# A cross-attention and MoE kernel on one core: first loads in four parts, states in two, and a new order of steps

## The chip, the cores and the metric

The kernel runs on one core of a Trainium2 chip. The metric is the device time of one execution in microseconds; several runs are made, and their median is compared.

## What is computed

Eight batches of x (8 heads, 512 tokens, 64 wide) and of a state (8 heads, 32 rows, 64 wide) attend to each other in both directions, and the two reads, laid one after the other, go through a two-layer network with a leaky activation:

```python
# x: (8, 8, 512, 64), state: (8, 8, 32, 64)
scores  = x @ state.T / 8;    xread = softmax(scores) @ state     # tokens read the states
scores2 = state @ x.T / 8;    sread = softmax(scores2) @ x        # states read the tokens
rows = concat([xread, sread], tokens)                             # (8 * 544, 512)
h = rows @ w_in                                                   # 512 -> 2048
g = max(h, 0) + alpha * min(h, 0)
out = g @ w_out                                                   # 2048 -> 512
```

## The kernel before

TensorE (PE) is given every matmul, VectorE (DVE), ScalarE (ACT) and GpSimd (POOL) share the rest, and SyncE (SP) issues most DMAs. Each engine works through its own list in order. These lists are written out in full: the text `ORDER` (lines 18 to 99) holds some 1,100 steps, a name and its numbers with points between, and the loop at lines 767 to 769 calls the function of each step in turn. A step's letters name its engine (`a`, `v`, `p`), and a last digit from 0 to 5 names the PSUM bank (one of six) that its result takes.

**The weights of the first product are folded into the states.** Since xread = a @ state, rows @ w_in = a @ (state @ w_in). A step `m.b.f` (line 517) multiplies batch b's states by the f-th quarter of w_in, and `mo` copies it out as f16. A step `F.b.jc` (line 550) is then one of 16 groups of 128 columns of h for the 512 tokens of batch b: two matmuls of 128 x 512. `N.b.jc` (line 606, ScalarE) takes relu(-h), `G.b.jc` (line 611, VectorE) adds (1 - alpha) times that to h, which gives g. Batch 8 in these names is the states' own rows.

**The second product.** For batch 0 it is plain: `S.0.q.j` (line 619) is two matmuls of 128 x 512 of output rows q, and `O` stores them. For batches 1 to 8 it is one level of a Strassen-like scheme with seven products: `P.b.p.i.c` (line 707) is four matmuls of 128 x 256 of product p, `U.b.i.c` (line 683, GpSimd) makes the sums of g that products 3, 5, 6 and 7 need, `W` the sums of the weights, `K` keeps a partial result, `Q.b.th.dh` (line 741) adds and stores a quarter; its output tiles `osb` have four buffers.

**Attention.** `sc` computes the scores of a batch with the states on the rows, `tm` the maximum over tokens, `te` the exponential, `tn` the norm, `tt` the transposition by DMA on SP, `rd` and `rdo` the states' reads. `sb` (line 346) transposes the scores in blocks of 32, `smax`, `ssh`, `sexp`, `ssum`, `snorm` and `wb` make the tokens' softmax, which `F` multiplies. For batches 2 to 7 `lx` loads x through GpSimd's queue with a cast to f16 and `xd` transposes it by DMA; for batches 0 and 1 TensorE transposes it (`xt`, copied out by `xo`).

**The opening.** Batch 0 goes in two halves of tokens, j = 0 and 1. `load_x0` loads each half as f32 on SP's queue, two DMAs of 512 KB; four steps `cx.j.g` cast a half's four heads to f16. `tsc` computes token scores of batch 0 directly, from the block-diagonal `st_pairs` that `sbd` fills; `at` and `ao` transpose the finished weights. `stc`, `stt`, `sto` cast, transpose and copy out batch 0's states; `lst` loads the states of batches 1 to 7 with one DMA, `str.i` transposes half i of them (0: batches 1 to 4's front part, 1: the rest), `sro.i` copies it out. `oma` transposes alpha and takes 1 - alpha. The first four column groups of batch 0 are computed by half: `f.0.pair.j`, four matmuls of 256, `n`, and `g` twice. `Z.k.n` (line 232) is a fill: n matmuls on a constant pattern into bank k whose result nothing reads. `wi` and `wo` load quarters of w_in and w_out through GpSimd's queue.

Of the kernel before, what the change touches and what calls it, by code (L numbers as in the profile page):

```python
# [29 lines left out]
S.0.3.3 F.0.9.4 m.1.2 F.0.12.1 ssh.p.1 sexp.1 G.0.10 S.0.2.5 S.0.1.5 ssum.1.s N.0.9 G.0.9 F.0.13.3 S.0.3.5 mo.1.2.a  # L30
m.1.3 N.0.12 G.0.12 S.0.3.4 F.0.15.4 tn.1.1.a N.0.13 G.0.13 F.0.14.1 S.0.1.4 S.0.3.6 S.0.1.6 W.2.0.p S.0.2.4 N.0.15
snorm.p.1 wb.1 F.1.3.3 G.0.15 S.0.2.6 F.1.7.4 tn.1.0.a W.2.1.p N.0.14 G.0.14 mo.1.3.a N.1.3 G.1.3 N.1.7 G.1.7 xd.2
tt.0 S.0.3.7 O.0.3.a F.1.12.1 N.1.12 G.1.12 F.1.1.3 N.1.1 W.4.1.p F.1.9.0 G.1.1 N.1.9 G.1.9 tt.1 S.0.2.7 O.0.2.a
F.1.2.4 N.1.2 G.1.2 F.1.10.1 N.1.10 S.0.1.7 sc.2 O.0.1.a tm.2 sb.2 m.2.2.3.2 mo.2.2.a.0 W.4.0.p rd.0.0 G.1.10
mo.2.2.a.1 F.1.0.4 N.1.0 rdo.0.a W.3.1.p lx.3 S.0.0.6.5 nb.2.a F.1.8.3 N.1.8 G.1.0 smax.2 te.2.0 F.1.4.2 S.0.0.7 G.1.8
te.2.1 F.1.5.0 N.1.5 S.0.0.5 G.1.5 F.1.11.1 N.1.11 S.0.0.2 S.0.0.4 S.0.0.3 G.1.11 N.1.4 G.1.4 m.2.1 mo.2.1.a F.1.6.4
N.1.6 G.1.6 F.1.15.3 N.1.15 G.1.15 F.1.13.0 N.1.13 S.0.0.0 F.1.14.1 N.1.14 W.3.0.p S.0.0.1 O.0.0.a ssh.p.2 sexp.2 xd.3
U.1.1.0.p G.1.13 P.1.1.0.1.2 P.1.1.1.1 m.3.2 m.2.3.4.3 mo.2.3.a.1 mo.2.3.a.0 G.1.14 m.3.0.5.0 ssum.2.1 P.1.1.0.0
U.1.2.0.p mo.3.0.a.0 P.1.1.1.0 K.1.1.a P.1.2.0.0.3 snorm.v.2 wb.2 P.1.2.1.0 P.1.2.0.1 U.1.1.1.p U.1.2.1.p P.1.2.1.1
mo.3.2.a P.1.6.1.0 mo.3.0.a.1 m.3.3.4.5 mo.3.3.a.1 mo.3.3.a.0 rd.1.1 Q.1.0.0 sc.3 tm.3 m.4.0.0.5 mo.4.0.a.0 sb.3  # L40
P.1.6.0.0 mo.4.0.a.1 rdo.1.a F.2.6.4 N.2.6 G.2.6 F.2.13.3 N.2.13 P.1.6.0.1 P.1.6.1.1 F.2.0.0 F.2.12.5 F.2.8.1 G.2.13
K.1.2.a P.1.5.1.0 N.2.0 N.2.12 G.2.12 G.2.0 P.1.5.1.1 P.1.5.0.0 N.2.8 G.2.8 nb.3.a te.3.0 F.2.2.4 N.2.2 G.2.2 te.3.1
lx.4 F.2.3.3 smax.3 F.2.15.5 N.2.15 F.2.14.0 G.2.15 N.2.3 U.1.3.0.p U.1.3.1.p P.1.7.1.0.1 F.2.7.4 N.2.7 U.1.4.0.p
P.1.7.0.1 N.2.14 m.6.0 mo.6.0.a G.2.3 P.1.7.0.0 F.2.9.5 G.2.14 P.1.7.1.1 P.1.5.0.1 N.2.9 G.2.7 G.2.9 F.2.5.3 K.1.4.a
ssh.p.3 F.2.11.0 N.2.5 N.2.11 F.2.4.4 U.1.4.1.p N.2.4 P.1.3.0.0 F.2.1.5 xd.4 tsum.2 tn.2.1.p sexp.3 tsum.3 Q.1.1.1
G.2.5 N.2.1 G.2.4 U.2.1.1.p P.1.4.1.0 tn.2.0.a P.1.4.0.1 G.2.11 P.1.4.0.0 m.5.0.3.4 m.4.3 mo.5.0.a.1 mo.5.0.a.0
mo.4.3.a P.1.3.1.1 tt.2 ssum.3.0 tn.3.1.a P.1.3.0.1 P.1.4.1.1 P.2.1.1.1.4 F.2.10.3 N.2.10 G.2.1 P.2.1.1.0 m.3.1
tn.3.0.p mo.3.1.a snorm.v.3 P.1.3.1.0 P.2.1.0.1 Q.1.0.1.a P.2.1.0.0 K.2.1.a Q.1.1.0 m.4.2.5.0 m.4.1.1.2 G.2.10 wb.3
sc.4 sb.4 tm.4 rd.2.3 mo.4.2.a.1 mo.4.2.a.0 U.2.2.1.p mo.4.1.a.0 tt.3 U.2.1.0.p U.2.2.0.p F.3.10.0 N.3.10 G.3.10
P.2.6.0.1 P.2.6.1.1 F.3.15.5 mo.4.1.a.1 lx.5 rdo.2.a N.3.15 G.3.15 F.3.14.1 F.3.8.2 N.3.14 G.3.14 F.3.0.3 N.3.0 G.3.0  # L50
N.3.8 G.3.8 F.3.12.0 N.3.12 G.3.12 nb.4.a P.2.6.1.0 F.3.2.5 N.3.2 G.3.2 F.3.13.1 P.2.6.0.0 K.2.2.a F.3.4.3 N.3.13
G.3.13 F.3.1.2 P.2.5.1.0 xd.5 N.3.4 F.3.9.0 N.3.9 G.3.9 G.3.4 te.4.1 P.2.5.0.0 P.2.5.1.1 F.3.7.5 U.2.3.1.p U.2.3.0.p
N.3.1 G.3.1 P.2.7.1.1.1 P.2.5.0.1 F.3.6.0 P.2.7.1.0 P.2.7.0.0 N.3.7 G.3.7 U.2.4.1.p te.4.0 smax.4 U.2.4.0.p K.2.4.a
N.3.6 G.3.6 m.5.3.3.2 mo.5.3.a.0 m.5.2 mo.5.2.a rd.3.5 rdo.3.v P.2.7.0.1 Q.2.1.1 F.3.3.3 N.3.3 ssh.p.4 G.3.3 lx.6
F.3.11.0 N.3.11 P.2.3.0.1 G.3.11 F.3.5.5 N.3.5 P.2.3.1.1 U.3.3.0.p P.2.3.0.0 G.3.5 mo.5.3.a.1 sexp.4 U.3.1.1.p
m.7.0.3.0 sc.5 P.2.3.1.0 Q.2.0.1.a mo.7.0.a.1 mo.7.0.a.0 tm.5 P.2.2.1.0.2 ssum.4.5 P.2.2.0.1 P.2.2.0.0 m.7.3.4.0
mo.7.3.a.1 mo.7.3.a.0 P.2.4.0.1 P.3.2.0.0.3 P.2.2.1.1 nb.5.a te.5.1 te.5.0 P.2.4.1.0 P.2.4.0.0 P.3.2.1.0 P.2.4.1.1
tsum.4 tn.4.0.a tn.4.1.a tt.4 P.3.2.0.1 snorm.v.4 wb.4 F.4.11.0 N.4.11 F.4.13.4 P.3.1.0.0.5 P.3.1.0.1 Q.2.1.0 sb.5
G.4.11 Q.2.0.0 xd.6 P.3.1.1.1 N.4.13 G.4.13 F.4.4.1 N.4.4 U.3.1.0.p G.4.4 U.3.2.0.p P.3.2.1.1 P.3.1.1.0 smax.5 K.3.1.a
Q.3.0.0 F.4.10.0 m.6.1.2.4 N.4.10 mo.6.1.a.1 mo.6.1.a.0 G.4.10 U.3.2.1.p m.5.1 P.3.6.1.0 tsum.5 F.4.5.1 N.4.5 G.4.5  # L60
U.3.3.1.p F.4.9.4 N.4.9 F.4.1.2 N.4.1 G.4.9 F.4.2.3 P.3.6.0.0 F.4.14.0 P.3.6.1.1 F.4.15.1 G.4.1 N.4.2 N.4.14 U.3.4.0.p
ssh.p.5 U.3.4.1.p G.4.2 mo.5.1.a G.4.14 N.4.15 P.3.7.1.0.4 G.4.15 F.4.3.2 P.3.7.0.0 N.4.3 G.4.3 P.3.6.0.1 K.3.2.a
F.4.0.3 N.4.0 sc.6 sb.6 rd.4.0 rdo.4.a m.7.2.1.2 P.3.5.1.0 mo.7.2.a.1 P.3.5.0.1 F.4.8.0 N.4.8 sexp.5 lx.7 tm.6 G.4.0
# [736 lines left out]
```

## Time and profile before

| | |
|---|---|
| median of 3 runs | 214.46 us (214.04 to 214.86) |
| the profiled execution, its own time | 214.07 us |
| its span, first to last instruction | 212.0 us |
| busy: TensorE, VectorE, GpSimd, ScalarE | 203.3, 174.2, 179.1, 152.6 us |
| granted TensorE clock | 1.00 |
| HBM read, written | 17.31 MB, 8.91 MB |

The busy time of an engine is the union of its instructions; matmuls are pipelined and overlap, so a busy TensorE can still have small gaps between matmuls. The 2 us between the span and the execution's own time lie outside the first and last instruction. A line `L556` is line 556 of the kernel; `idle before` is the time that the engine stood still ahead of an instruction, with what released it.

### The profile page before, as it was taken

How to read it: one execution, taken by the hardware profiler on the slowest of the kernel's cores; microseconds unless marked ns; L12 is line 12 of the kernel's file. 1: busy time of each engine (PE TensorE's matmuls, PEld its weight loads, DVE VectorE, ACT ScalarE, POOL GpSimd, SP SyncE). 2: the span in 40 equal slices, each digit the busy share in tenths (PEclk: the TensorE clock that was granted, in tenths of full speed). 3: DMA queues.
4: the chain of work that ended last, by engine and by line, in shares of the span. 5: the costliest groups of instructions: out<-in, count | busy, mean ns of one | idle time of the engine just before them, and what ended most of it. 6: DMA issues, size and time to landing. Idle time of an engine off the chain costs nothing.

```text
span 212.0 us, 5108 instructions
## 1 busy us (share of the span) xinstructions
PE 203.3 (96%) x2034; PEld 137.7 (65%) x2034; DVE 174.2 (82%) x260; ACT 152.6 (72%) x300; POOL 179.1 (84%) x111
## 2 busy tenths in 40 slices
...
GB/s 159 219 204 207 206 204 89 160 165 90 152 105 89 106 84 135 110 134 143 183 117 49 103 106 192 3 51 40 162 53 49 99 3 49 49 53 49 74 124 102
DMA packets 43975, 23.70 MB, mean 112 GB/s; under 512 B 22192, under 2 KB 43440, under 8 KB 43952
## 3 DMA queue, kind: packets, MB, share of 16 engines
...
q10 hardware_dynamic: 272, 0.07, 0.1%
...
HBM read 17.31 MB, written 8.91 MB: 124 GB/s over the span
## 4 chain that ended last, share of the span: by engine, by line
PE 88%; DMA 7%; ACT 2%; issue 1%; SPq 0%; DVE 0%; ACTq 0%
PE h L556 25%; PE px L715 23%; PE pv L715 12%; PE o L626 6%; PE py L715 5%; PE m_ps L507 4%; PE h L565 3%; PE fill L236 3%; DMA xT<-xg 2%; DMA x<-in_x_dram 2%; PE sr_ps L480 2%; DMA out_dram<-oq 2%; DMA e2T<-e 1%; PE sc L314 1%; PE xT_ps L299 1%; PE h L578 1%
## 5 line engine op out<-in xcount | busy, mean ns | idle before, releaser
L612 DVE SCALAR_TENSOR_TENSOR g<-neg,oma_sb,h 128x512 f16<-128x512 f32 (+1 forms) x140 | 92.7, 708 | 11.6 <-ACT neg L609 11.1
L609 ACT ACTIVATE neg<-h 128x512 f32<-128x512 f32 (+1 forms) x140 | 75.0, 585 | 23.0 <-PE h L556 14.4
L556 PE MATMUL h<-aT,m 128*128 128x512 f16 x248 | 67.2, 379 | 0.1
L715 PEld LDWEIGHTS <-gsum 128*128 128x128 f16 x480 | 46.1, 98 | 16.8 <-issue 1.8
L715 PEld LDWEIGHTS <-g 128*128 128x128 f16 x360 | 35.0, 98 | 9.1 <-issue 0.9
L694 POOL TENSOR_TENSOR gsum<-g 128x1024 f16<-128x1024 f16 (+1 forms) x16 | 32.0, 2009 | 4.2 <-DVE g L612 3.6
L694 POOL TENSOR_TENSOR gsum<-g,g 128x1024 f16<-128x1024 f16 (+1 forms) x16 | 32.0, 2004 | 3.9 <-DVE g L612 3.8
L556 PEld LDWEIGHTS <-m 128*128 128x128 f16 x248 | 23.7, 98 | 15.5 <-issue 0.8
L694 POOL TENSOR_TENSOR gsum<-gsum,g 128x1024 f16<-128x1024 f16 (+1 forms) x16 | 32.1, 2006 | 1.1
L715 PE MATMUL px<-ws,gsum 128*128 128x256 f16 x240 | 32.6, 273 | 0.0
L694 POOL TENSOR_TENSOR gsum<-g,gsum 128x1024 f16<-128x1024 f16 (+1 forms) x16 | 31.9, 2005 | 0.1
L731 ACT COPY kept<-px 128x512 f32<-128x512 f32 (+1 forms) x22 | 12.7, 577 | 14.0 <-PE px L715 13.7
L533 ACT CAST m<-m_ps 128x512 f16<-128x512 f32 x36 | 20.0, 613 | 1.8 <-PE m_ps L507 1.5
L384 POOL TENSOR_TENSOR ts<-ts,mx 128x1024 f32<-128x1024 f32 x7 | 13.4, 1908 | 5.4 <-DVE mx L379 5.4
L715 PE MATMUL px<-w_out_sb,gsum 128*128 128x256 f16 x120 | 17.4, 273 | 0.0
L715 PE MATMUL pv<-ws,gsum 128*128 128x256 f16 x120 | 17.2, 273 | 0.0
L748 DVE TENSOR_TENSOR oq<-pv,kept 128x512 f32<-128x512 f32 (+1 forms) x16 | 10.5, 655 | 8.1 <-PE pv L715 6.7
L626 PE MATMUL o<-w_out_sb,g 128*128 128x512 f16 x64 | 17.1, 380 | 0.0
L715 PE MATMUL pv<-ws,g 128*128 128x256 f16 x120 | 16.9, 273 | 0.0
L715 PE MATMUL px<-w_out_sb,g 128*128 128x256 f16 x120 | 16.9, 273 | 0.0
L715 PE MATMUL py<-w_out_sb,g 128*128 128x256 f16 x120 | 16.2, 273 | 0.0
L531 ACT CAST m<-m_ps 128x1024 f16<-128x1024 f32 x12 | 12.4, 1032 | 1.3 <-PE m_ps L507 1.2
...
## 6 DMA issues: line engine op xcount, KB each, us to landing
...
xg<-in_x_dram POOLq DMA_DIRECT2D x7, 512.0 KB, 6.9
w_in_sb<-in_moe_w_in_dram POOLq DMA_DIRECT2D x4, 512.0 KB, 9.3
w_out_sb<-in_moe_w_out_dram POOLq DMA_DIRECT2D x4, 512.0 KB, 12.2
x<-in_x_dram SPq DMA_DIRECT2D x2, 512.0 KB, 5.3
...
```

The costliest lines, as they stand in the source:

```text
L384: engine(e).tensor_tensor(blocks(cols(live["ts", b], j, S)), blocks(scored(b, j)), over_blocks(cols(live["mx", b], j, S // N)), ALU.subtract,)
L507: nc.tensor.matmul(t[N * k : N * (k + 1), :], st_head(b, h)[64 * r : 64 * r + 64, :], w_in_sb[64 * r : 64 * r + 64, c, 512 * f : 512 * (f ...
L531: copier(e)(m_tile(b, f), t)
L533: copier(e)(m_tile(b, f)[:, g, :], t[g])
L556: nc.tensor.matmul(h.rearrange("p (r j s) -> p r j s", r=2, j=2), ms[b, f][:, g, 128 * j : 128 * (j + 1)], weights(b, g), start=(g == 0), ...
L609: nc.scalar.activation(neg, h, RELU, bias=0.0, scale=-1.0)
L612: nc.vector.scalar_tensor_tensor(g_tile(b, jc), negs.pop((b, jc)), oma_sb[:, jc : jc + 1], hs.pop((b, jc)), ALU.mult, ALU.add,)
L626: nc.tensor.matmul(outs[b, q], g_tile(b, jc)[:, 128 * q : 128 * (q + 1)], w_out_sb[:, jc, :], start=not begun and jc == 2 * jc2, stop=left ...
L694: engine(e).tensor_tensor(t, x(), y(), op)
L715: nc.tensor.matmul(pbanks[b, name][:, i, :], of(b, c)[:, j, 128 * i : 128 * (i + 1)], moving[:, 4 * c + j, :], start=not begun and j == 0, ...
L731: copier(e)(t, pbanks[b, "x"])
L748: nc.vector.tensor_tensor(osb, pbanks[b, name], kept[b, add], ALU.add)
```

## The change

- Each half of batch 0's x is loaded by two DMAs of four heads, 256 KB each, so four in all on the same queue. The cast `cx` can now also be placed on GpSimd (`copier("p")`).
- The load of the later states is cut in two steps, `lst.0` and `lst.1`; in the new order `lst.1` stands behind the last w_in quarter.
- Clearing alpha's rows and loading alpha become a step `la`, with the clearing on GpSimd instead of VectorE.
- `state_max` and `state_sum` take an engine, through two new step names that the new order does not use.
- Batch 0's second column pair (groups 2 and 3) is computed whole, as `F`, `N`, `G`, not by halves as `f`, `n`, `g`.
- The order is new throughout: every step has another place, many have another bank, and some another engine (for instance `sro` goes from ScalarE to VectorE, `sbd` from VectorE to ScalarE, one of batch 0's `snorm` from GpSimd to VectorE). There are 36 fill matmuls in 6 steps, where there were 42 in 16; 16 more at the start stay.

The order's first and last lines, and the code:

```diff
--- before.py
+++ after.py
 ORDER = """
-Z.0.3 stc.a stt.0 cx.0.1.v xt.0.0.1.1 xo.0.0.1.a wi.0 cx.0.0.v xt.0.0.0.2 xo.0.0.0.a sbd.0.v lst sbd.1.v Z.3.2 sto.a
-Z.3.2 Z.3.3 cx.1.0.v xt.0.1.0.3 cx.1.1.v tsc.0.1.4 tsc.0.0 smax.0.0 ssh.v.0.0 xo.0.1.0.a xt.0.1.1.5 xo.0.1.1.a Z.1.3
-Z.1.2 sc.0.0 sc.0.1 tsc.1.1.1 m.0.0.2.0 tsc.1.0 sexp.0.0 tm.0 smax.0.1 ssum.0.0 Z.3.3 mo.0.0.a.1 lx.1 Z.3.2 Z.3.2
-Z.3.3 ssh.v.0.1 str.1.3 nb.0.a te.0.1 Z.5.3 str.0.5 Z.4.3 Z.4.3 te.0.0 sexp.0.1 Z.4.2 mo.0.0.v.0 Z.4.3 wi.1 ssum.0.1
-wo.0 sro.0.a xt.1.0.0.4 snorm.p.0.0 at.0.0 ao.0.a wo.1 Z.1.3 tsum.0 snorm.p.0.1 xt.1.0.1.1 m.1.0 xt.1.1.0.2 sro.1.a
-wi.2 oma.a xo.1.0.0.v wi.3 xo.1.0.1.v xo.1.1.0.a f.0.0.0.5 xt.1.1.1.0 n.0.0.0 mo.1.0.v at.1.4 ao.1.v m.0.1.1.3
-tn.0.1.p mo.0.1.v.1 m.1.1 mo.1.1.a g.0.0.0.0 g.0.0.0.1 f.0.0.1.2 n.0.0.1 f.0.1.1.4 mo.0.1.a.0 n.0.1.1 f.0.1.0.3
-xo.1.1.1.v g.0.0.1.1 g.0.0.1.0 sc.1 tm.1 m.2.0.5.0 mo.2.0.a.1 mo.2.0.a.0 F.0.5.1 N.0.5 F.0.4.2 N.0.4 nb.1.a te.1.1
-g.0.1.1.0 g.0.1.1.1 G.0.5 S.0.3.0.0 wo.2 G.0.4 S.0.1.0.5 S.0.1.1 sb.1 F.0.7.4 N.0.7 G.0.7 F.0.6.1 wo.3 tn.0.0.p N.0.6
-S.0.3.1 G.0.6 n.0.1.0 g.0.1.0.0 S.0.2.2.2 S.0.3.2 te.1.0 S.0.1.2 S.0.2.0 g.0.1.0.1 m.0.2 S.0.2.3 S.0.1.3 smax.1
-mo.0.2.a F.0.8.4 N.0.8 G.0.8 W.1.1.p F.0.11.1 N.0.11 G.0.11 tsum.1 F.0.10.3 N.0.10 m.0.3 mo.0.3.a W.1.0.p lx.2 S.0.2.1
-...
-P.7.2.1.0.3 Q.7.1.1 P.7.2.0.1 P.7.2.0.0 P.7.3.0.1 P.7.2.1.1 U.8.1.0.p P.7.3.1.0 P.7.4.0.1 P.8.1.0.1 P.7.3.0.0 Q.7.0.0
-K.8.1.a P.7.4.1.1 U.8.2.0.p P.8.6.0.0 P.7.4.0.0 P.7.4.1.0 Q.7.1.0 U.8.1.1.p U.8.2.1.p P.8.6.0.1 K.8.2.v P.7.3.1.1
-P.8.7.0.0.5 P.8.5.0.1 P.8.5.0.0 K.8.4.a P.8.7.0.1 P.8.2.0.0 U.8.4.0.p Q.7.0.1.v P.8.3.0.0 Q.8.1.1 P.8.4.0.1 U.8.4.1.p
-P.8.4.0.0 Q.8.0.0 Q.8.1.0 P.8.3.0.1 Q.8.0.1.a
+cx.0.0.v stc.a stt.0 sbd.1.a xt.0.0.0.1 xo.0.0.0.a cx.0.1.v xt.0.0.1.2 cx.1.0.v xo.0.0.1.v xt.0.1.0.3 sbd.0.a
+tsc.0.0.4 tsc.0.1 cx.1.1.v xo.0.1.0.a xt.0.1.1.5 Z.1.3 sto.a sc.0.0 xo.0.1.1.a sc.0.1 smax.0.0 ssh.v.0.0 sexp.0.0
+tsc.1.1.1 wi.0 lst.0 tsc.1.0 lx.1 la tm.0 nb.0.a te.0.1 Z.2.9 m.0.0.2.3 smax.0.1 ssh.v.0.1 sexp.0.1 oma.a str.0.0
+te.0.0 Z.5.6 sro.0.v mo.0.0.a.0 Z.5.9 wi.1 ssum.0.1 wo.0 mo.0.0.a.1 wi.2 xt.1.1.0.5 tsum.0 m.2.0.4.1 m.1.0 mo.1.0.a
+xt.1.0.1.0 mo.2.0.a.1 xo.1.0.1.a xt.1.1.1.2 Z.3.3 snorm.p.0.1 ssum.0.0 mo.2.0.v.0 snorm.v.0.0 at.1.3 ao.1.v xt.1.0.0.4
+xo.1.1.0.v m.1.1 mo.1.1.a xo.1.1.1.v xo.1.0.0.v wi.3 at.0.1 lst.1 ao.0.v f.0.0.1.3 m.0.1.0.5 sc.1 F.0.3.2 sb.1 tm.1
+F.0.2.4 n.0.0.1 wo.1 mo.0.1.a.0 mo.0.1.a.1 N.0.2 F.0.5.1 g.0.0.1.1 N.0.3 N.0.5 g.0.0.1.0 f.0.0.0.0 G.0.2 wo.2 nb.1.a
+wo.3 te.1.1 te.1.0 Z.5.6 F.0.6.5 S.0.1.0.3 N.0.6 G.0.3 tn.0.1.p W.1.0.p S.0.3.0.4 m.0.2 mo.0.2.a S.0.1.1 F.0.7.2 N.0.7
+S.0.3.1 G.0.5 G.0.6 n.0.0.0 tn.0.0.p smax.1 ssh.p.1 F.0.9.1 N.0.9 m.0.3 mo.0.3.a G.0.7 g.0.0.0.0 lx.2 xd.2 F.0.8.5
+g.0.0.0.1 F.0.4.2 N.0.4 G.0.9 tsum.1 N.0.8 m.1.2 mo.1.2.a G.0.4 str.1.0 F.0.13.1 G.0.8 S.0.1.3 sexp.1 F.0.11.2 S.0.1.2
+...
+F.8.3.1 N.8.3 G.8.3 N.8.8 G.8.8 N.8.7 G.8.7 P.7.2.0.1 P.7.2.0.0 P.7.5.1.0 P.7.5.0.1 G.8.14 F.8.11.1 N.8.11 P.7.5.1.1
+P.7.5.0.0 P.7.7.1.0.0 U.7.3.1.p P.7.7.0.1 G.8.11 P.7.7.0.0 P.7.7.1.1 P.7.2.1.1 U.7.4.0.p P.8.1.0.0.4 K.7.4.v Q.7.1.1
+Q.7.0.0 U.7.4.1.p P.7.3.0.0 P.7.3.0.1 P.8.1.0.1 P.7.4.1.1 P.7.3.1.0 P.7.4.1.0 P.7.4.0.0 K.8.1.a P.7.4.0.1 Q.7.1.0
+U.8.1.1.p U.8.2.1.p P.8.6.0.1 U.8.1.0.p U.8.2.0.p P.8.6.0.0 U.8.3.1.p P.8.7.0.1.2 P.7.3.1.1 K.8.2.v P.8.5.0.0
+P.8.5.0.1 K.8.4.v Q.7.0.1.a U.8.3.0.p P.8.7.0.0 Q.8.1.1 P.8.2.0.0.1 P.8.2.0.1 Q.8.0.0 P.8.4.0.1 P.8.4.0.0 Q.8.1.0
+U.8.4.0.p P.8.3.0.0 U.8.4.1.p P.8.3.0.1 Q.8.0.1.a
...
@@ -146,6 +145,8 @@
         return ps.tile(shape, dtype, name=name, tag="two", bufs=1)
 
     def copier(e):
+        if e == "p":
+            return nc.gpsimd.tensor_copy
         return nc.scalar.copy if e == "a" else nc.vector.tensor_copy
 
     def engine(e):
@@ -167,9 +168,12 @@
         xgs[0] = att.tile([128, H, 2, 2, D], F16, name="xg_0", tag="xg", bufs=3)
         for j in range(2):
             t = att.tile([128, H, 2, D], F32, name=f"x0_{j}", tag="ts", bufs=2)
-            nc.sync.dma_start(
-                t, x[0, :, 256 * j : 256 * (j + 1), :].rearrange("k (p r) d -> p k r d", r=2)
-            )
+            for g in range(2):
+                heads = slice(4 * g, 4 * g + 4)
+                nc.sync.dma_start(
+                    t[:, heads, :, :],
+                    x[0, heads, 256 * j : 256 * (j + 1), :].rearrange("k (p r) d -> p k r d", r=2),
+                )
             x0s.append(t)
 
     def x0_cast(j, g, e):
@@ -183,13 +187,16 @@
     st0_32 = consts.tile([128, 2, D], F32)
     nc.scalar.dma_start(st0_32, rows[:n0, :].rearrange("(g p) d -> p g d", p=128))
     alpha_rows = consts.tile([128, N], F32)
-    nc.vector.memset(alpha_rows, 0.0)
-    for q in range(4):
-        nc.sync.dma_start(
-            alpha_rows[N * q : N * q + n_jc, :],
-            moe_alpha.rearrange("(jc q p) -> q jc p", q=4, p=N)[q],
-        )
     alpha_sb = consts.tile([128, N], F32)
+
+    def load_alpha():
+        nc.gpsimd.memset(alpha_rows, 0.0)
+        for q in range(4):
+            nc.sync.dma_start(
+                alpha_rows[N * q : N * q + n_jc, :],
+                moe_alpha.rearrange("(jc q p) -> q jc p", q=4, p=N)[q],
+            )
+
     pattern = consts.tile([128, 256], F16)
     nc.gpsimd.iota(
         pattern, pattern=[[37, 256]], base=-4800, channel_multiplier=29,
@@ -199,10 +206,10 @@
     make_identity(nc, ident)
     st = consts.tile([128, n_j, D], F16)
 
-    def load_states():
+    def load_states(i):
         nc.gpsimd.dma_start(
-            st.rearrange("p (i j) d -> p i j d", i=2),
-            rows[n0:, :].rearrange("(i p j) d -> p i j d", i=2, j=w_st),
+            st[:, w_st * i : w_st * (i + 1), :],
+            rows[n0:, :].rearrange("(i p j) d -> i p j d", i=2, j=w_st)[i],
         )
 
     w_in_sb = consts.tile([128, n_c, d_ff], F16)
@@ -374,9 +381,9 @@
             return cols(live["ts", b], j, S)
         return live["tsc", j].rearrange("p r h n -> p (r h n)")
 
-    def state_max(b, j=None):
+    def state_max(b, j=None, e="v"):
         soft_tiles(b)
-        nc.vector.tensor_reduce(
+        engine(e).tensor_reduce(
             cols(live["mx", b], j, S // N), blocks(scored(b, j)), AX.X, ALU.max
         )
 
@@ -392,14 +399,14 @@
         ts = cols(live["ts", b], j, S)
         nc.scalar.activation(ts, ts, EXP, bias=0.0, scale=scale)
 
-    def state_sum(b, jk):
+    def state_sum(b, jk, e="v"):
         j = None if b else jk
         if jk == "s":
             live["r1", b] = att.tile([128, 2 * S // N], F32, name=f"r1_{b}", tag="r1", bufs=2)
         elif b:
             live["r1", b] = single(jk, f"r1_{b}", [128, 2 * S // N], F32)
         r1 = cols(live["r1", b], j, S // N)
-        nc.vector.tensor_reduce(r1, blocks(cols(live["ts", b], j, S)), AX.X, ALU.add)
+        engine(e).tensor_reduce(r1, blocks(cols(live["ts", b], j, S)), AX.X, ALU.add)
         nc.vector.reciprocal(r1, r1)
 
     def state_norm(e, b, j=None):
@@ -752,11 +759,11 @@
     steps = {
         "lst": load_states, "wi": load_w_in, "wo": load_w_out, "lx": load_x,
         "stc": first_states_cast, "stt": first_states_transposed, "sto": first_states_out,
-        "oma": one_less_alpha, "sbd": first_states_paired, "str": states_transposed, "sro": states_out,
+        "la": load_alpha, "oma": one_less_alpha, "sbd": first_states_paired, "str": states_transposed, "sro": states_out,
         "xd": x_transposed_dma, "xt": x_transposed, "xo": x_out, "sc": scores, "cx": x0_cast, "tsc": token_scores,
         "at": tokens_transposed, "ao": tokens_out,
         "sb": score_blocks, "smax": state_max, "ssh": state_shift, "sexp": state_exp,
-        "ssum": state_sum, "snorm": state_norm, "wb": weights_back,
+        "ssum": state_sum, "smx": lambda e, b: state_max(b, None, e), "ssm": lambda e, b: state_sum(b, "s", e), "snorm": state_norm, "wb": weights_back,
         "tm": token_max, "nb": token_shift, "te": token_exp, "tsum": token_sum, "tn": token_norm,
         "tt": token_transposed, "rd": state_reads, "rdo": state_reads_out,
         "m": state_w_in, "mo": state_w_in_out,
```

128 lines of the change are left out of this document (63 added, 65 removed).

## The prediction

> **What bounds it.** I read the page first (busy shares, chain), then busy time by stretches, the waits of TensorE, and the timeline of the opening and the tail.
>
> ```profile
> PE 203.3 (96%) x2034; PEld 137.7 (65%) x2034; DVE 174.2 (82%) x260; ACT 152.6 (72%) x300; POOL 179.1 (84%) x111
> ...
> PE 88%; DMA 7%; ACT 2%; issue 1%; SPq 0%; DVE 0%; ACTq 0%
> ```
> ```profile
> 0.00:22.00 22.00, 19.22 (x251) 12.53 (x252) 13.52 (x30) 13.03 (x25) 12.26 (x21) 1.00 1.12 198
> 22.00:200.00 178.00, 176.57 (x1719) 118.95 (x1718) 157.76 (x225) 138.50 (x273) 162.28 (x87) 1.00 0.50 101
> ```
> ```profile
> PE sr_ps L480 <- DMA e2T<-e: 1.0, 1, 1.0
> ...
> PE sc L314 <- DMA xT<-xg: 0.4, 1, 0.4
> ```
> The columns of the stretches are length, then busy time of PE, PEld, DVE, ACT and POOL, the granted clock, the DMA share and GB/s. From 22 to 200 us TensorE is busy for 176.57 of 178.00 us, and the 1.43 us that it is not are the two waits quoted: one for a transposed e2 (1.0), one for a transposed x (0.4). So from 22 us on the kernel is TensorE's own work. The change leaves that work alone: the same products, and batch 0's second column pair costs four 512-wide matmuls where it had eight of 256. So the span moves by what TensorE loses: idle time and fills (matmuls on a pattern, useful to nobody) in the opening, waits after it, and the tail. The first 22 us count 19.22 busy, but much of that is fill:
>
> ```profile
> L236 PE MATMUL fill<-pattern 128*128 128x256 f16 x58 | 10.5, 306 | 1.8 <-POOL pattern L194 1.2
> ```
> The 58 fills fall to 52 (16 at the start stay, 42 become 36), but a fill only stands where TensorE would wait anyway; what counts is when real work can start.
>
> **The opening, first half.** These rows carry it:
>
> ```profile
> 4.22 0.78 POOL L212 DMA_DIRECT2D w_in_sb<-in_moe_w_in_dram  x1
> ...
> 5.44 0.88 DVE L176 CAST xg<-x 128x512 f16<-128x512 f32 x2 [4.27 <-DMA x<-in_x_dram]
> ...
> 7.18 0.76 DVE L176 CAST xg<-x 128x512 f16<-128x512 f32 x2 [0.36 <-DMA x<-in_x_dram]
> ...
> 8.69 0.69 DVE L379 TENSOR_REDUCE mx<-tsc 128x16 f32<-128x512 f32 x1 [0.74 <-PE tsc L353]
> ...
> 13.64 0.58 PE L248 MATMUL st_ps<-ident,st 128*64 128x128 f16 x14
> ```
> ```profile
> L426 DVE TENSOR_REDUCE nb<-sc 128x2 f32<-128x1024 f32 x8 | 9.7, 1213 | 1.4 <-PE sc L314 1.3
> ...
> L346 DVE STREAM_TRANSPOSE ts<-sc 128x1024 f32<-128x1024 f32 x7 | 8.7, 1238 | 0.0
> ...
> L379 DVE TENSOR_REDUCE mx<-tsc 128x16 f32<-128x512 f32 x2 | 1.4, 686 | 0.7 <-PE tsc L353 0.7
> L533 DVE CAST m<-m_ps 128x512 f16<-128x512 f32 x2 | 1.4, 684 | 0.0
> L402 DVE TENSOR_REDUCE r<-ts 128x16 f32<-128x512 f32 x2 | 1.4, 682 | 0.1
> L384 DVE TENSOR_TENSOR ts<-tsc,mx 128x512 f32<-128x512 f32 x2 | 1.3, 660 | 0.0
> L304 DVE COPY xT<-xT_ps 128x512 f16<-128x512 f16 x3 | 1.3, 422 | 2.1 <-PE xT_ps L299 2.1
> ```
> Today both halves of x land as a whole, at 5.4 and 7.2 us. In four loads on the same queue I put the quarters at about 4.5, 5.4, 6.3 and 7.2 (the second and fourth at the landings of today, the others half-way). The first cast then starts 0.9 us sooner, but the last one no sooner, and from there VectorE is the chain. Its list after the last cast (7.65) is max and shift of column 0 (0.69+0.66), 0.25 of waiting for the scores, the token max (1.21), max and shift of column 1 (0.69+0.66), alpha's transpose (0.2, an estimate: it is a fortieth of L346's elements), the copy of the states to the front of batch 4 (0.8, an estimate: 1.75 times the 0.42 of a 512-wide copy, and a little for its strided rows), two sums with their reciprocals (0.93+0.11+0.93), one m cast (0.68), the norm of column 0 (0.66: it leaves GpSimd for VectorE) and five copies of 0.42. That is 10.6, so it ends near 18.25 and TensorE's first whole column group F.0.3 starts near 18.4. Today the comparable point, F.0.5, is at 21.89; but by then TensorE has also done three column-half steps (3 x 0.43) and 14 transposes of states (0.55) that the changed order does later. 21.89-1.85 = 20.05: the changed order is 1.65 us ahead here, and waits for one GpSimd norm less. No cast goes to GpSimd: all four steps in the new order still name VectorE, so that part of the change is only an option, at nothing. Alpha's clearing moves to GpSimd, behind the issue of batch 1's x; its loads, on SP's queue behind the clearing, start where today's GpSimd issues the next weights, at 4.2 us; VectorE needs alpha at 11.8.
>
> **The opening, second half**, from F.0.3 to 29 us. Today:
>
> ```profile
> 21.89 1.04 PE L556 MATMUL h<-aT,m 128*128 128x512 f16 x4
> ...
> 22.81 1.76 PE L626 MATMUL o<-w_out_sb,g 128*128 128x512 f16 x6
> ...
> 24.41 1.03 PE L556 MATMUL h<-aT,m 128*128 128x512 f16 x4
> ...
> 25.27 2.32 PE L626 MATMUL o<-w_out_sb,g 128*128 128x512 f16 x10
> ...
> 27.52 0.41 PE L507 MATMUL m_ps<-w_in_sb,stT 64*32 64x512 f16 x8
> ...
> 27.95 1.04 PE L626 MATMUL o<-w_out_sb,g 128*128 128x512 f16 x4
> ...
> 29.07 1.47 PE L556 MATMUL h<-aT,m 128*128 128x512 f16 x6
> ```
> Two F's take 25.27-24.41 = 0.86, so 0.43 for a step of two 512-wide matmuls. From 21.89 to 29.07 stand 28 of these (6.0) and one m (0.35 to 0.43): 6.4 of 7.18, 0.8 lost. It works because S steps (output matmuls) fill the time in which VectorE makes g. The changed order takes F first, and both VectorE passes over batch 1's scores (1.24 + 1.21) before any g:
>
> ```profile
> L612 DVE SCALAR_TENSOR_TENSOR g<-neg,oma_sb,h 128x512 f16<-128x512 f32 x124 | 85.7, 738 | 7.1 <-ACT neg L609 6.7
> ```
> ```profile
> L609 ACT ACTIVATE neg<-h 128x512 f32<-128x512 f32 x124 | 69.5, 610 | 14.8 <-PE h L556 14.4
> L533 ACT CAST m<-m_ps 128x512 f16<-128x512 f32 x36 | 20.0, 613 | 1.8 <-PE m_ps L507 1.5
> ...
> L443 ACT ACTIVATE e<-sc,nb 128x512 f16<-128x512 f32 x16 | 11.0, 688 | 0.3
> ```
> So the first two halves of g come at 21.9, G.0.2 at 22.6, G.0.3 at 23.3. ScalarE's list, from 17.85: a negative (0.61), two m casts (to 19.65), three negatives (to 21.4), 0.27 and two exponentials (to 23.1), then the next. TensorE stands: F.0.5 waits for the second m cast (0.4 idle), after f.0.0.0 (20.6) come the six fills of step Z.5.6 (0.9), S.0.1.0 and S.0.3.0 wait for g (0.3), m.0.2 for the exponentials, F.0.4 for G.0.7 (26.7; 0.6 idle), m.1.2 for the cast of m.0.3 (27.65; 0.55 idle). By 29.05 it has done nine F, one f and four S (14 x 0.43 = 6.0), three m (1.05) and 14 transposes (0.55): 7.6 of 10.65, 3.0 lost against 0.8. So +2.2, and the two halves sum to +0.5. To 36 us the same walk meets another m (m.3.2, 0.4) behind ScalarE's casts: +0.4 (0 to 1.0). The later load of the second half of the states hides: it is issued ahead of the last three w_out loads and its transposes come at 28 us.
>
> **After the opening.** Between a transposed x's issue and its scores the new order puts 11 to 19 us of TensorE work where today's puts 3.5 to 9 (steps counted at the prices above), so I take out both waits quoted: -1.4. The change also replaces 175 us of order that today has no other wait. Below, there is nothing more to gain there; above, the bound is the wait of the GpSimd rival. I take +0.4.
>
> **The tail.**
> ```profile
> 203.72 0.68 DVE L746 COPY oq<-px 128x512 f32<-128x512 f32 x1
> ...
> 206.91 0.60 PE L715 MATMUL px<-w_out_sb,gsum 128*128 128x256 f16 x4
> ...
> 208.18 0.37 ACT L746 COPY oq<-px 128x256 f32<-128x256 f32 x1 [2.88 <-DMA out_dram<-oq]
> ```
> TensorE ends at 207.5, yet the last copy starts at 208.18: it waits for the buffer of the copy of 203.72, four outputs earlier. That copy moves to ScalarE and stands no longer behind a VectorE copy: -0.35 (0 to -0.6).
>
> **Sum:** +0.5+0.4-1.4+0.4-0.35 = -0.45 us. The profiled execution took 214.07 us for its span of 212.0; the median of the runs is 214.46. 214.46-0.45 = 214.0.
>
> **A page that speaks against it.** Splitting costs nothing in my sum, since today's two loads land 1.8 us apart though each is 5.3 us under way: they overlap.
>
> ```profile
> x<-in_x_dram SPq DMA_DIRECT2D x2, 512.0 KB, 5.3
> ```
> The Trainium skill, "DMA: Bandwidth & Descriptors", section Bandwidth, says to batch loads to 1 MiB, with about 2 us fixed for each. Were that cost paid one after the other, an estimate from it, two loads more would put the last quarter 4 us later and the sum at +3.5; the overlap in the row speaks against it.
>
> **Rivals.**
> *The head start holds* (0.32): S steps slip in as today, and the second half loses 0.8 to 1.9 instead of 3.0. Then -1.65 to -2.55 of it comes on top: 211.5 to 212.9. For: VectorE reaches G.0.5 some 0.7 us sooner with batch 1's transposition already done. Against: the named waits follow from the lists.
>
> *GpSimd becomes the end* (0.21). Place: the sums for the last product steps.
> ```profile
> L694 POOL TENSOR_TENSOR gsum<-gsum,g 128x1024 f16<-128x1024 f16 x14 | 29.8, 2128 | 0.9
> ...
> L694 POOL TENSOR_TENSOR gsum<-g,g 128x512 f16<-128x512 f16 x2 | 2.3, 1156 | 0.0
> ```
> From U.7.4.0 on the new order leaves GpSimd two sums of 2.13 and eight of 1.156, 13.5 us, beside 22 product steps of four 256-wide matmuls (0.435 each, 9.6 us); today it is one and eight, 11.4 us, beside 29 steps, 12.6. It has to be 3.9 us ahead of its place there. Followed back to U.7.1.1, I find some 0.4 us to spare at P.8.7.0.1; each microsecond of lateness beyond that is one at the end. GpSimd is busy for 162 of 178 us, so 2 to 3 late is possible: +1.6 to +2.6 in place of the 0.4: 215.2 to 216.4 and, over 215.53, slower.
>
> *Alpha or the first loads come late* (0.07): VectorE stands in order at alpha's transpose; if alpha lands after 11.8, everything behind moves by the delay. 1.5 to 2.5 us: 215.6 to 216.6.
>
> *The clock* (0.04). The rows show 1.00 granted in every stretch. Between the first fills and 9.3 us the new order has 3 fills where today's has 15, with real matmuls every half microsecond or so. If the clock went to half there, the matmuls to 12 us would take twice their time, 1.5 us more on the way to VectorE: 215.6. The Trainium skill, "TensorE: Matmul & The Clock Gate", section Part 1, states that an idle window of about 3.4 us halves it; no stretch here is that idle.
>
> **Numbers.** The forecast, within 0.5% (213.39 to 215.53; about what a measurement of this kernel can tell from no change), has 0.36, and its own range is 213.4 to 215.5. Faster is the first rival, 0.32; slower the other three, 0.32. The range 212.0 to 216.5 leaves out the far parts of both.
>
> **What would show it.** Right: VectorE without gaps from 7.7 to 24 us; F.0.3 near 18.4; fills of Z.5.6 near 20.8 and 3 us lost before 29; no wait for e2T or xT; the last copy within 0.3 us of TensorE's end. Wrong: F.0.3 after 19.5 (loads or alpha); TensorE waiting for gsum after 190 us; or TensorE dense from 19 us on.

## The result: 220.24 us, and the profile after

The changed kernel took 220.24 us (median of 4 runs, 219.57 to 220.54), the kernel before 214.47 us beside it (4 runs, 214.04 to 214.86): a ratio of 1.0268, 95% interval 1.025 to 1.0286. The forecast was 214.0 us with a range of 212.0 to 216.5; the kernel is 2.7% slower and outside of that range. The profiled execution took 220.13 us for a span of 218.0. All ratios and intervals here leave out runs more than 1.5% above the fastest of the same kernel, while medians count every run; that matters for one kernel below, three loads with the sum in SBUF, where 3 of 12 runs are left out.

The changed kernel's page (busy time; the granted clock in 40 slices of 5.45 us; the chain that ended last by engine):

```profile
PE 204.9 (94%) x2024; PEld 138.2 (63%) x2024; DVE 178.3 (82%) x262; ACT 149.1 (68%) x295; POOL 179.2 (82%) x113
...
PEclk9757999999999999999999999999999999999998
...
PE 85%; DMA 5%; DVE 4%; ACT 3%; issue 1%; SPq 1%; DVEq 0%; ACTq 0%
```

By stretches (length, then busy time of PE, PEld, DVE, ACT, POOL, the granted clock, DMA share, GB/s):

```profile
0.00:22.00 22.00, 14.69 (x161) 9.67 (x162) 10.06 (x19) 8.53 (x19) 6.84 (x16) 0.77 1.02 176
22.00:200.00 178.00, 175.95 (x1737) 115.99 (x1735) 161.44 (x231) 138.50 (x273) 160.21 (x89) 1.00 0.52 101
```
```profile
5.00:10.00 5.00, 1.44 (x17) 1.01 (x18) 1.64 (x4) 1.21 (x3) 1.38 (x2) 0.84 1.16 196
10.00:15.00 5.00, 2.80 (x58) 1.98 (x57) 2.03 (x4) 2.08 (x4) 0.00 (x0) 0.50 1.37 205
```

The kernel before, from 5 to 15 us:

```profile
5.00:10.00 5.00, 4.12 (x76) 2.71 (x76) 3.41 (x8) 2.49 (x6) 0.75 (x2) 1.00 1.27 226
10.00:15.00 5.00, 4.66 (x63) 3.02 (x64) 4.83 (x11) 4.12 (x9) 1.80 (x2) 1.00 1.35 203
```

From 22 us on TensorE is nearly as dense as before (2.05 us idle against 1.43). The time went in the opening: 14.69 us busy where it was 19.22, and a clock of 0.77. Between 5 and 15 us TensorE, VectorE and ScalarE mostly stand, while the DMA engines are about as full as before (a share adds up the time of packets that overlap, so it can pass 1). What they stand for is told by VectorE's timeline and by TensorE's waits (us in total, times, longest):

```profile
4.45 1.44 DVE L180 CAST xg<-x 128x512 f16<-128x512 f32 x2 [3.31 <-DMA x<-in_x_dram]
9.09 0.43 DVE L180 CAST xg<-x 128x512 f16<-128x512 f32 x1 [3.21 <-DMA x<-in_x_dram]
...
12.32 0.43 DVE L180 CAST xg<-x 128x512 f16<-128x512 f32 x1 [2.47 <-DMA x<-in_x_dram]
```
```profile
PE xT_ps L306 <- DVE xg L180: 5.8, 3, 3.2
PE h L563 <- DVE an L413: 1.3, 1, 1.3
...
PE h L563 <- ACT neg L616: 0.2, 1, 0.2
```

The first two quarters of x are cast from 4.45 and 5.1 us on, about where I put them (4.5 and 5.4); the third comes at 9.1 and the fourth at 12.3, where I had 6.3 and 7.2. From the last cast on the kernel runs as listed, only later and at first at half the clock (0.50 from 10 to 15 us). TensorE's timeline has the marks (the first row begins with F.0.3, the second is f.0.0.0, the third Z.5.6, the fourth begins with F.0.13; the last two rows are the tail):

```profile
24.99 1.52 PE L563 MATMUL h<-aT,m 128*128 128x512 f16 x6
26.34 0.60 PE L585 MATMUL h<-aT,m 128*128 128x256 f16 x4
26.78 0.82 PE L243 MATMUL fill<-pattern 128*128 128x256 f16 x6
...
34.29 0.61 PE L563 MATMUL h<-aT,m 128*128 128x512 f16 x2
```
```profile
213.22 1.04 PE L722 MATMUL px<-w_out_sb,gsum 128*128 128x256 f16 x8
...
214.34 0.37 ACT L753 COPY oq<-px 128x256 f32<-128x256 f32 x1 [3.39 <-PE px L722]
```

### The profile page after: what moved, and what is told of

Its sections match the earlier page's. It is cut to its first block, busy times and chain, and to the rows that moved or that the text cites. A ratio compares the mean times of both kernels' runs of the same rounds, so it can differ in the third digit from the quotient of the medians.

```text
span 218.0 us, 5090 instructions
## 1 busy us (share of the span) xinstructions
PE 204.9 (94%) x2024; PEld 138.2 (63%) x2024; DVE 178.3 (82%) x262; ACT 149.1 (68%) x295; POOL 179.2 (82%) x113
## 3 DMA queue, kind: packets, MB, share of 16 engines
q0 software_dynamic: 11792, 8.09, 26.4%
## 4 chain that ended last, share of the span: by engine, by line
PE 85%; DMA 5%; DVE 4%; ACT 3%; issue 1%; SPq 1%; DVEq 0%; ACTq 0%
PE px L722 24%; PE h L563 24%; PE pv L722 12%; PE py L722 6%; DMA x<-in_x_dram 5%; PE m_ps L514 4%; PE o L633 4%; PE h L572 3%; PE fill L243 2%; PE sr_ps L487 2%; PE sc L321 1%; DVE g L619 1%; ACT m L540 1%; ACT neg L616 1%; PE xT_ps L306 1%
## 5 line engine op out<-in xcount | busy, mean ns | idle before, releaser
L619 DVE SCALAR_TENSOR_TENSOR g<-neg,oma_sb,h 128x512 f16<-128x512 f32 (+1 forms) x142 | 93.9, 708 | 8.8 <-ACT neg L616 8.0
L563 PE MATMUL h<-aT,m 128*128 128x512 f16 x252 | 67.9, 379 | 1.7 <-DVE an L413 1.3
L701 POOL TENSOR_TENSOR gsum<-g,g 128x1024 f16<-128x1024 f16 (+1 forms) x16 | 32.0, 2007 | 10.1 <-DVE g L619 8.7
L563 PEld LDWEIGHTS <-m 128*128 128x128 f16 x252 | 24.0, 98 | 19.5 <-DVE an L413 1.8
L722 PE MATMUL px<-ws,gsum 128*128 128x256 f16 x240 | 31.8, 273 | 0.0
L540 ACT CAST m<-m_ps 128x512 f16<-128x512 f32 x34 | 19.0, 600 | 1.2 <-PE m_ps L514 1.2
L738 ACT COPY kept<-px 128x512 f32<-128x512 f32 (+1 forms) x19 | 11.0, 581 | 11.2 <-PE px L722 11.2
L722 PE MATMUL pv<-ws,gsum 128*128 128x256 f16 x120 | 16.4, 273 | 0.0
L722 PE MATMUL px<-w_out_sb,g 128*128 128x256 f16 x120 | 16.2, 273 | 0.0
L538 ACT CAST m<-m_ps 128x1024 f16<-128x1024 f32 x13 | 13.4, 1029 | 3.1 <-PE m_ps L514 3.1
L413 POOL TENSOR_TENSOR an<-ts,r 128x512 f16<-128x512 f32 (+1 forms) x2 | 3.0, 1482 | 14.8 <-DVE r L460 14.4
```

The source lines that it names most:

```text
L538: copier(e)(m_tile(b, f), t)
L540: copier(e)(m_tile(b, f)[:, g, :], t[g])
L563: nc.tensor.matmul(h.rearrange("p (r j s) -> p r j s", r=2, j=2), ms[b, f][:, g, 128 * j : 128 * (j + 1)], weights(b, g), start=(g == 0), ...
L619: nc.vector.scalar_tensor_tensor(g_tile(b, jc), negs.pop((b, jc)), oma_sb[:, jc : jc + 1], hs.pop((b, jc)), ALU.mult, ALU.add,)
L701: engine(e).tensor_tensor(t, x(), y(), op)
L722: nc.tensor.matmul(pbanks[b, name][:, i, :], of(b, c)[:, j, 128 * i : 128 * (i + 1)], moving[:, 4 * c + j, :], start=not begun and j == 0, ...
```

## The experiments

My theory after the result: in four parts, x shares the DMA engines with the weights that GpSimd issues from 1.65 us on, and so comes late; the half clock makes it worse. The rivals: each load's fixed cost is paid one after the other (the reading that the prediction dismissed); or the new order itself is slow.

**Is it the loads?** The changed kernel with x in two loads, and the kernel before with four (the first of these edits, shortened at the dots; the second is its reverse):

```diff
-            for g in range(2):
-                heads = slice(4 * g, 4 * g + 4)
-                nc.sync.dma_start(t[:, heads, :, :], x[0, heads, ...])
+            nc.sync.dma_start(t, x[0, :, ...])
```

Two loads in the changed kernel: 

> The changed kernel with batch 0's x in two loads of 512 KB again; all else as changed. Split theory (four smaller loads let the weights' queue in between, so the last quarter lands at 12.3 us): the last half lands near 7.2 us, GpSimd's queue moves its first packets only near 5.9 us, no clock of a half after 8 us, and the time falls by 5 to 7 us, to 213.4 to 215. Order theory (the new places cost the time, the late x only hides it): x lands early but the time stays above 217. GpSimd-list theory (the cut states' load and alpha's clearing start the weights earlier, which crowds x out): the last half still lands after 9 us and the time stays above 217.

Four loads in the kernel before: 

> The kernel before with only the four loads of 256 KB added. Split theory: the last quarter lands between 10 and 12.5 us, and the time rises by 3.5 to 6 us, to 218 to 220.5. Order theory and GpSimd-list theory: the last quarter lands by 7.5 us and the time stays within 1 us of 214.5.

Two loads in the changed kernel took 214.38 us (10 runs; ratio to the kernel before 1.0011, 0.9995 to 1.0027). Four loads in the kernel before took 220.75 us (1.0313, 1.0255 to 1.037). So the split is the whole loss, in either order, and the new order, GpSimd's list with it, has no net part in it. VectorE's timeline of the first and of the second:

```profile
5.72 0.95 DVE L177 CAST xg<-x 128x512 f16<-128x512 f32 x2 [4.59 <-DMA x<-in_x_dram]
7.41 0.43 DVE L177 CAST xg<-x 128x512 f16<-128x512 f32 x1 [0.73 <-DMA x<-in_x_dram]
8.09 0.42 DVE L177 CAST xg<-x 128x512 f16<-128x512 f32 x1
```
```profile
5.09 0.96 DVE L179 CAST xg<-x 128x512 f16<-128x512 f32 x2 [3.92 <-DMA x<-in_x_dram]
9.86 0.43 DVE L179 CAST xg<-x 128x512 f16<-128x512 f32 x1 [2.97 <-DMA x<-in_x_dram]
12.95 0.43 DVE L179 CAST xg<-x 128x512 f16<-128x512 f32 x1 [2.67 <-DMA x<-in_x_dram]
```

The DMA view from 4 to 6 us shows what differs (queue, packets, MB, share; q1 is SP's queue with x, q0 GpSimd's with the weights). First four loads (the changed kernel), then two:

```profile
q1 hardware_dynamic: 517, 0.25, 55.7%
q0 software_dynamic: 122, 0.12, 48.1%
```
```profile
q1 hardware_dynamic: 1190, 0.60, 116.4%
q0 software_dynamic: 8, 0.01, 4.5%
```

**Cost of a load, or sharing?** The changed kernel, with the last cast given to GpSimd ahead of the first weights, which so wait for all of x:

```diff
-tsc.0.0.4 tsc.0.1 cx.1.1.v xo.0.1.0.a
+tsc.0.0.4 tsc.0.1 cx.1.1.p xo.0.1.0.a
```

> The changed kernel with the last quarter's cast on GpSimd, ahead of its first weight load, so that no weight is issued before all of x has landed; four loads kept. Split theory by sharing (the loss is in the turns that the weights' queue takes): the last quarter lands near 7 us, though the weights come 4 to 6 us later and the time is no better than 218. Rival, a fixed cost of each load paid one after the other: the quarters still land 3 us apart and the last after 11 us.

It took 219.59 us in one run, but x came early: VectorE casts three quarters at 4.29, 5.13 and 6.10, GpSimd the fourth at 6.90.

```profile
4.29 0.43 DVE L180 CAST xg<-x 128x512 f16<-128x512 f32 x1 [3.15 <-DMA x<-in_x_dram]
...
17.53 0.21 DVE L279 STREAM_TRANSPOSE alpha_sb<-alpha_rows 128x32 f32<-128x32 f32 x1 [6.03 <-DMA alpha_rows<-in_moe_alpha_dram]
```
```profile
PE m_ps L514 <- DMA w_in_sb<-in_moe_w_in_dram: 3.0, 1, 3.0
...
PE st_ps L255 <- DMA st<-in_state_dram: 1.3, 1, 1.3
```

Four loads on one queue are thus about 0.9 us apart when alone: a cost for each, paid one after the other, is not the cause; sharing is what is left, and is tested once more below. The Trainium skill, "DMA: Bandwidth & Descriptors", section Queues, rings and completion order, says that each DMA engine takes turns between the queues that have work, a packet at a time. The changed kernel agrees from 7 to 9.5 us, when both queues have work throughout:

```profile
q0 software_dynamic: 368, 0.33, 81.4%
q1 hardware_dynamic: 360, 0.18, 35.0%
```

That is nearly one packet for one, but x's packets are about half as large, so x gets a third of the bytes, some 0.07 MB per us. The prediction did not weigh this. In the run that held the weights back the gain was spent elsewhere: alpha's clearing stood behind the held weights on GpSimd, and VectorE waited 6.03 us for alpha, the mechanism of my third rival.

**The clock.** The changed kernel with two more fills in the gaps (24 and 14 matmuls):

```diff
-xt.0.0.1.2 cx.1.0.v
+xt.0.0.1.2 Z.5.24 cx.1.0.v
-xo.0.1.0.a xt.0.1.1.5
+xo.0.1.0.a Z.0.14 xt.0.1.1.5
```

> The changed kernel with 38 more fill matmuls where TensorE waits for x (24 after the second quarter's transposes, 14 before the last's). Clock theory (the half clock from 8.4 to 18.6 us is a second loss on top of the late x): full clock from 5 us on, F.0.3 starts 1 to 1.5 us sooner than 25.0, and the time falls by 0.8 to 1.6 us, to 218.6 to 219.4. Rival, VectorE alone sets the opening: the clock is full but the time stays within 0.4 us of 220.2.

218.12 us (4 runs; 1.0192, 1.0157 to 1.0227). Stretches and casts:

```profile
5.00:10.00 5.00, 3.82 (x42) 3.15 (x43) 1.08 (x3) 1.21 (x3) 1.49 (x3) 1.00 1.05 171
10.00:15.00 5.00, 4.11 (x78) 3.10 (x76) 2.45 (x5) 2.08 (x4) 0.00 (x0) 1.00 1.38 206
```
```profile
12.40 0.43 DVE L180 CAST xg<-x 128x512 f16<-128x512 f32 x1 [2.40 <-DMA x<-in_x_dram]
...
22.83 1.52 PE L563 MATMUL h<-aT,m 128*128 128x512 f16 x6
```

x is as late, the clock is full, and from the last cast to F.0.3 pass 10.43 us where the changed kernel needs 12.67 (24.99 - 12.32). So the half clock costs 2.2 us in the opening; from the medians it is 2.1, from the ratios 1.6. At the least it is 0.8: one of the changed kernel's own runs shows a clock of 1.000 and took 219.57, the other three 220.34 in the median. That run is still 1.45 us above the median with the fills, and no profile of it is kept, so the price stays between 0.8 and 2.2 us.

**Why do the weights come in early?** First came three loads, and then four on two queues (SP's and ScalarE's, the quarters in turn, with batch 0's states issued ahead of them):

```diff
-            for g in range(2):
-                heads = slice(4 * g, 4 * g + 4)
+            for heads in (slice(0, 8),) if j == 0 else (slice(0, 4), slice(4, 8)):
```

> The changed kernel with column half 0 of x in one load of 512 KB and half 1 in two of 256 KB. Two-in-flight theory (the engines work off the first two loads of SP's queue before the weights' queue gets a turn, and share from the third on): the first two land by 6.5 us, the third lands after 8.5 us, near 10. Size theory (any load under 512 KB lets the weights in as soon as it is done): the second and the third both come late, the second after 7.5 us. Time between 216 and 219.5 by both.

One run, 214.0 us, with the third load on time (last cast at 7.34), against both theories of the expectation. I took that as the end of the theories that make a third load late. It was too quick, as the same loads show further down.

```diff
-                nc.sync.dma_start(
+                (nc.sync, nc.scalar)[g].dma_start(
```

> The changed kernel with its four loads kept, but one of each pair on ScalarE's queue, behind the load of batch 0's states, and one on SP's. Two-in-flight theory: no queue has more than two or three loads, so all quarters land by 7.5 us or one late near 8.5, and the time is 213.5 to 215.5. Size theory: quarters still land up to 12 us and the time stays above 218.

216.39 us (7 runs; 1.0082, 1.0057 to 1.0108): three quarters are cast from 4.41, 6.00 and 6.54 on, the last from 9.14. Better than one queue, worse than two loads, and the time is that of neither theory.

Then the number of loads and the size of the first were set against each other, with these heads (half 0, then half 1):

```diff
-(slice(0, 8),) if j == 0 else (slice(0, 4), slice(4, 8))
+(slice(0, 8),) if j == 0 else (slice(0, 4), slice(4, 6), slice(6, 8))   # four, the first 512 KB
+(slice(0, 4), slice(4, 8)) if j == 0 else (slice(0, 8),)                # three, the first 256 KB
```

> The changed kernel, still with four loads of x, but first half 0 whole (512 KB), then heads 0 to 3 of half 1 (256 KB), then heads 4 and 5, then 6 and 7 (128 KB each). Open is what lets the weights' queue in at 4.0 to 4.4 us when x comes in four quarters, while with two or three loads it got its first packets at 5.9. Theory A (the fourth load): any fourth load lets the weights in before the third is done; the weights start near 4.4 us, the last cast starts at 9 us or later, and the time is 216 to 219 us. Theory B (a small first load): what counts is that the first load is small, so that it is done early; with a whole half in front all casts start by 7.6 us and the time is 213.8 to 214.6 us.

> The changed kernel with three loads of x the other way round: half 0 in two quarters of 256 KB, then half 1 whole (512 KB). Theory A (the fourth load): three loads all come on time, as in the run with the whole half first: last cast by 7.8 us, 213.8 to 214.6 us. Theory B (a small first load): the first quarter is done near 3.8 us, the weights' queue starts near 4.4 us, and half 1 lands after 9 us: 216 to 219 us.

Four loads with a large first one: 217.35 us (4 runs; 1.0151, 1.0133 to 1.0169), last cast at 10.32. Three with a small first one: 220.46 us (4 runs; 1.0281, 1.0261 to 1.0302), as slow as the change itself:

```profile
4.04 0.45 DVE L179 CAST xg<-x 128x512 f16<-128x512 f32 x1 [2.90 <-DMA x<-in_x_dram]
...
11.12 0.43 DVE L179 CAST xg<-x 128x512 f16<-128x512 f32 x1 [5.97 <-DMA x<-in_x_dram]
11.79 0.42 DVE L179 CAST xg<-x 128x512 f16<-128x512 f32 x1
```

So the count does not decide alone: three loads can be as bad as four. Nor does the first load's size: with a large one the last cast was still late. The packets of the profiled executions nearly order it by one quantity, how much of x is not yet moved when the weights' first packet starts:

| kernel | first cast starts, us | weights' first packet, us | x left then, MB | last cast starts, us |
|---|---|---|---|---|
| changed, weights held until all of x is in | 4.29 | 9.17 | 0 | 6.90 |
| changed, three loads, first 512 KB | 5.33 | 5.97 | 0.08 | 7.34 |
| changed, two loads, a second time | 5.27 | 5.91 | 0.09 | 7.71 (half 1 in at 7.03) |
| before (two loads) | 5.44 | 5.92 | 0.09 | 7.52 (half 1 in at 7.18) |
| changed, two loads | 5.72 | 5.77 | 0.10 | 8.09 (half 1 in at 7.41) |
| two queues, a second time | 4.38 | 5.57 | 0.12 | 8.60 |
| three loads, first 512 KB, a second time | 5.44 | 5.60 | 0.14 | 8.79 |
| changed, two queues | 4.41 | 5.43 | 0.19 | 9.14 |
| four loads, first 512 KB | 5.18 | 5.26 | 0.21 | 10.32 |
| three loads, first 256 KB | 4.04 | 4.49 | 0.47 | 11.79 (half 1 in at 11.12) |
| changed (four of 256 KB) | 4.45 | 4.24 | 0.51 | 12.32 |
| before, four of 256 KB | 5.09 | 4.34 | 0.50 | 12.95 |
| changed, with more fills | 4.27 | 4.20 | 0.51 | 12.40 |

Left to themselves, the weights come in between 0.75 us ahead of the first cast and 1.2 us behind it, so near the first landing, early when that load is small. What is left of x then shares with them and moves at 0.04 to 0.08 MB per us (0.51 MB from 4.24 to 12.3, 0.14 from 5.60 to 8.8), where in two loads it moved 0.60 MB in the 2 us from 4 to 6. That is a regularity of twelve executions, not yet a mechanism.

**A test of it.** Four quarters, but the weights only a little later: alpha first, the first quarter cast on GpSimd ahead of the first weights, and one later sum written to SBUF (more on it below).

```diff
-cx.0.0.v stc.a stt.0
+la cx.0.0.p stc.a stt.0
-wi.0 lst.0 tsc.1.0 lx.1 la tm.0
+wi.0 lst.0 tsc.1.0 lx.1 tm.0
-lx.4 ssum.2.0 snorm.v.2
+lx.4 ssum.2.s snorm.v.2
```

> The changed kernel with its four quarters of x, but alpha is cleared and loaded first, and the first quarter is cast on GpSimd ahead of the first weights, which so are issued at about 4.9 us instead of 1.65; and the column sums of batch 2 come from the copy in SBUF. If the weights' queue, once it runs, is what makes the quarters late: with 1.6 us from issue to first packet, as in the run that held the weights back, the weights come in at about 6.5, when no more than the last few packets of x are left; the quarters are cast from 4.3 to 7.3 us, alpha causes no wait, and the time is 212.3 to 213.3 us, the level of two loads with that sum (213.1) or a little under it, with up to 0.6 us of TensorE waiting for the first weights and for the states. If the quarters are late by themselves, whatever the weights do: last cast after 9 us and 215 to 218 us.

214.32 us (12 runs; 1.0002, 0.9986 to 1.0019). The weights' first packet starts at 6.69 with nothing of x left, VectorE's casts run to 7.8, alpha comes in time:

```profile
6.87 0.90 DVE L180 CAST xg<-x 128x512 f16<-128x512 f32 x1
```
```profile
PE xT_ps L306 <- DMA xg<-in_x_dram: 2.3, 1, 2.3
...
PE st_ps L255 <- DMA st<-in_state_dram: 0.2, 1, 0.2
```

The quarters are not late by themselves; the reading holds. The time I missed by a microsecond: what VectorE gained, batch 1's x lost, which stands behind the weights on the same queue and now comes 2.3 us after TensorE wants it. I had counted the weights and the states there, not that load. The profiled execution, with 215.75 us, is the slowest of the twelve; that this wait makes the whole microsecond in the others is not shown.

**A faster version.** The new wait for `an` (1.3 us) goes back to a sum of batch 2's softmax: `ssum.2.0` writes its result to PSUM bank 0, and the buffer there is free only once ScalarE has copied the products `m` out of it. Timeline of the changed kernel with two loads:

```profile
50.78 2.05 ACT L537 CAST m<-m_ps 128x512 f16<-128x512 f32 x4
...
52.92 1.23 DVE L406 TENSOR_REDUCE r<-ts 128x32 f32<-128x1024 f32 x1 [2.00 <-ACT m L537]
...
55.86 0.60 PE L560 MATMUL h<-aT,m 128*128 128x512 f16 x2 [1.30 <-DVE an L410]
```

`ssum.2.s` (the last two lines of the diff above) writes the same sums to SBUF, which is what the expectations mean by the sum from SBUF. In the version with it and two loads the sum waits for nothing:

```profile
49.52 1.22 DVE L406 TENSOR_REDUCE r<-ts 128x32 f32<-128x1024 f32 x1
```

The expectations for that sum with two loads, with two queues, and with three loads:

> The changed kernel with two loads of x again, and batch 2's sum written to SBUF instead of PSUM bank 0 (one step, ssum.2.0 made ssum.2.s). Bank theory (with two loads the rest of the change has no net gain since at 52 us VectorE's sum of batch 2 waits for ScalarE's fourth cast, which frees bank 0, and TensorE then waits 1.3 us for the weights): the sum starts near 51 us instead of 52.9, the wait of 1.3 goes, and the time falls by 1.0 to 1.6 us below the same kernel without it, to 212.8 to 213.4. Rival, ScalarE's or VectorE's load is the bound there: the wait moves to another step and the time stays within 0.3 us of 214.4.

> Four loads on two queues and batch 2's sum in SBUF together. Two-in-flight and bank theories: both gains add, 212.3 to 213.6. Size theory: above 217.

> The changed kernel with three loads (half 0 whole, half 1 in two quarters) and the column sums of batch 2 taken from their copy in SBUF. If the two gains add (three loads came out at 214.0 in one run against 214.4 for two; the sum from SBUF took 1.2 us off the kernel with two loads): 212.5 to 213.3 us, the fastest of all. If three loads gain nothing over two, 213.1.

Two loads: 213.12 us (6 runs, 212.7 to 213.9; 0.9945, 0.9924 to 0.9965), about half a per cent faster than the kernel before. Two queues: 215.49 us (12 runs; 1.0049, 1.003 to 1.0068), again the time of neither theory. Three loads: 215.49 us (12 runs, 212.77 to 216.61; 1.0021, 0.9994 to 1.0047): my expectation of 212.5 to 213.3 rested on the single run of 214.0, one of the good ones. Its last cast was at 8.79 here. With two loads and that sum, VectorE's last cast, F.0.3 on TensorE, and the wait that follows in the place of `an`:

```profile
7.71 0.42 DVE L177 CAST xg<-x 128x512 f16<-128x512 f32 x1
```
```profile
18.23 1.52 PE L560 MATMUL h<-aT,m 128*128 128x512 f16 x6
```
```profile
PE h L560 <- DVE aT L418: 0.9, 1, 0.9
```

## Why the prediction was wrong, point by point

**The step that failed** is "In four loads on the same queue I put the quarters at about 4.5, 5.4, 6.3 and 7.2 (the second and fourth at the landings of today, the others half-way)". The first stood (4.45), the second was cast at 5.1; the third and fourth were 2.8 and 5.1 us late. I reasoned from the overlap of today's two loads with each other and asked nothing of the weights' queue that had been waiting since 1.65 us. "Splitting costs nothing in my sum" fell with it: with two loads the same order took 214.38 us, 0.4 from the forecast, so the split that I put at nothing cost 5.9 us (220.24 against 214.38; 5.5 by the ratios). It did not fall by a fixed cost paid one after the other: held free of the weights, the four quarters come about 0.9 us apart. The cost of about 2 us that I quoted stands in another section of that page of the Trainium skill, "Anatomy of one DMA — SWDGE (gpsimd) path", and is a fit for loads issued from GpSimd, while x is issued from SP. Of my signs of being wrong, F.0.3 after 19.5 us is the one that showed.

**First half of the opening.** F.0.3 started at 24.99, not 18.4. Against the version with two loads and the sum in SBUF, which ran at full clock, the 6.76 us (24.99 - 18.23) are 4.61 of the last cast (12.32 - 7.71) and 2.15 of the list behind it (12.67 against 10.52). That version's 18.23 is close to my 18.4, in part by luck: its last cast ended 0.5 us later than I had (8.13 against 7.65), and from there to F.0.3 took 10.1 us instead of 10.75, though the copy of the states was 1.05 to 1.09 us, not 0.8 (the row is the changed kernel's):

```profile
18.69 1.09 DVE L289 COPY stT<-st_ps 128x896 f16<-128x896 f16 x1 [1.33 <-PE st_ps L255]
```

Its gain over before was thus there to be had; the loads took it.

**Second half.** F.0.3 to F.0.13 took 9.30 us (24.99 to 34.29); my walk, in which F.0.13 ends at 29.05, had 10.2. The fills of Z.5.6 followed f.0.0.0 as said. Of the 0.9 us less, 0.4 lie ahead of these fills: they started 1.8 us after F.0.3 (26.78), where I had 2.2 (20.6), since F.0.5 did not stand the 0.4 us that I had it wait. Where the other 0.5 lie is not settled.

**After the opening.** Both DMA waits, for e2T and for xT, are gone, as predicted. "I take +0.4" for new waits was too little: 1.3 for `an` and 0.2 for `neg`, 1.5 together. The case that GpSimd becomes the end did not come: TensorE waits for no gsum anywhere, and the stretch to 200 us is full:

```profile
190.00:200.00 10.00, 10.00 (x93) 8.90 (x91) 5.76 (x11) 2.31 (x7) 9.47 (x6) 1.00 0.15 53
```
From F.0.13 to the end went 183.71 us; the prediction had 182.95.

**The tail.** TensorE ends at 214.26 and the last copy starts at 214.34, released by TensorE: within the 0.3 us said.

**The sum.** 6.6 late at F.0.3, -0.9, +0.76: 6.45 us, the distance of the span of 218.0 from the predicted 211.55.

**The rivals.** The clock had 0.04 and a price of 1.5 us; it did go to half, for 0.8 to 2.2, but as a consequence of the late x, not by itself. I quoted an idle window of about 3.4 us (the Trainium skill, "TensorE: Matmul & The Clock Gate", section Part 1) as speaking against it; the longest wait was 3.2, and the clock fell with TensorE busy for 1.44 of 5 us, so the measurement decides: here it took no stretch of 3.4 us without work. Alpha and the first loads had 0.07 together and 1.5 to 2.5 us. Alpha came in time (its transposition at 17.15 waited for nothing), the loads did not, and by twice that delay, so that even this rival's 216.6 was 3.6 short. Some sums of the rivals do not come out as written: the head start's losses of 0.8 to 1.9 instead of 3.0 give 211.8 to 212.9, the GpSimd rival ends at 216.2, and the times of the last two are 0.1 lower; none of this bears on the miss.
